# A gated linear recurrence and a SiLU network on one core: the state's product with values as weights, and two reorderings at the start

## The chip, the cores and the metric

The kernel runs on one core of a Trainium2 chip. The metric is the time of one execution on the device in microseconds (us). The kernel before has a median of 665.35 us over three runs (663.98 to 667.26). The profile is that of another execution of the same program: 663.49 us in all, with a span of 661.8 us on the core.

Five engines work side by side, each with its own list of instructions in order: TensorE (PE: matrix products; PEld is its weight load), VectorE (DVE), ScalarE (ACT), GpSimd (POOL) and SyncE (SP), which here only starts transfers. Transfers (DMA) are started on the queues of SyncE, GpSimd and ScalarE, and run beside all of them.

## The reference

Two parts stand one behind the other. First a recurrence in each of 4 x 8 batches and heads, over 768 steps, with a complex state of 48 x 48 that is multiplied by a gate for each row and takes up the outer product of key and value; the output is the query times the real part of the state.

```python
batch, n_heads, seq, head_dim = (4, 8, 768, 48)
...
for t in range(S):
    ar, ai = (a_re_n[:, :, t, :, None], a_im_n[:, :, t, :, None])   # |a| capped at 0.999
    new_re = ar * S_re - ai * S_im
    new_im = ar * S_im + ai * S_re
    kv = np.einsum('bhd,bhe->bhde', k[:, :, t], v[:, :, t])
    S_re, S_im = (new_re + kv, new_im)
    y[:, :, t] = np.einsum('bhd,bhde->bhe', q[:, :, t], S_re)
```

Then a network over the 3072 rows of 384 that the heads make together:

```python
h = x @ w_in                      # (3072, 384) x (384, 2048)
g = h * (1.0 / (1.0 + np.exp(-h)))
return (g @ w_out).astype(np.float32)
```

## The kernel before

The recurrence is worked out in chunks of 128 steps. There are 24 chunks, counted n = 0 to 23: four sequences with six chunks each, so chunk n goes on from chunk n - 4, and chunks 20 to 23 are the last of their sequences. Two chunks make a pair p, and a pair is one step of the main loop: beside the attention of pair p stand the two network products of pair p - 1 (`h`, line 689, and `r`, the product into `o`, line 781) and the gates of pair p + 1.

In a chunk, keys and queries are turned by the running phase of the gates and scaled by their running decay, so that a head has 96 numbers (cosine and sine part) for each time: `kr` and `qr`. With their transposes `kT` and `qT` the kernel makes the weights inside the chunk (`a`, masked to `w`), and the output `y` from two products: values by weights, and the state that was carried in by queries. The state at the end of the chunk is a product over time of `kr` and `v`, added to the state before and multiplied by the decay of the whole chunk.

```python
def output(n):                       # n >= 4; line 592
    ps = p_m.tile([C, HH, C], F32, tag="m", name=f"y{n}")
    for hp in range(HH):             # HH = 4 couples of heads, C = 128
        for r in range(2):           # one head to each half of the partitions
            h = 2 * hp + r
            cols = ds(h * D, 64 if h + 1 < H else D)      # D = 48
            to = ps[64 * r:64 * r + (64 if h + 1 < H else D), hp]
            nc.tensor.matmul(to, lhsT=v_[:, cols], rhs=x["w", h // HH][:, h % HH], ...)
            if carried:
                nc.tensor.matmul(to, lhsT=x["S"]...[:, cols], rhs=x["qT"][:, h], ...)
    ...                              # copied into xT (ScalarE); six small transfers place
                                     # the last two heads' rows in xT, the network's input

def state(n):                        # line 658
    if place(n)[1] == NCH - 1:       # last chunk of its sequence: no state wanted
        return
    ps = p_m.tile([D2, H, D], F32, tag="m", name=f"s{n}")            # D2 = 96
    for h in range(H):
        nc.tensor.matmul(ps[:, h], lhsT=x["kr"][:, h].rearrange("p c d -> p (c d)"),
                         rhs=x["v"][:, h], start=True, stop=True)
    x["s"] = ps
    if n >= STRAIGHT:                # STRAIGHT = 4
        carried_on(n)

def carried_on(n):                   # line 671
    new = att.tile([D2, H, D], F32, tag="S", name=f"S{n + B}", bufs=5)     # B = 4
    by = decs[:, n].unsqueeze(2).to_broadcast([D2, H, D])
    if "S" in x:
        nc.vector.tensor_tensor(out=new, in0=ps, in1=x["S"], op=ALU.add)
        nc.vector.tensor_tensor(out=new, in0=new, in1=by, op=ALU.mult)
    else:
        nc.vector.tensor_tensor(out=new, in0=ps, in1=by, op=ALU.mult)
    X[n + B]["S"] = new
```

The first operand named (`lhsT`) is the stationary one, which is loaded as weights; the second (`rhs`) is moved through. The decay of the whole chunk is the last row of `eq`; it goes to a DRAM array `ends` and comes back, turned, to the tile `decs` on two times 48 partitions (line 511). The transposes of keys and queries are made by VectorE in blocks of 32 x 32 (`sq`, line 560), and twelve transfers put the blocks in their places (`T<-sq`, line 565, half of them on SyncE's queue and half on GpSimd's).

The chunks of the first three pairs, the loads and conversions of the network's weights and the first pairs of the network stand in a list written by hand. A weight's block is loaded raw (as pairs of words; `F`, line 185), and is converted by ScalarE (`R`, the low word, line 218) and VectorE (`H` the high word, `J` both joined); there are four raw buffers. The part of the list that matters here:

```python
... carried:5 r:1 L:5 g:13 r:1 H:1 J:1 F:1 H:1 phase:4 F:1 H:1 R:1 R:1 g:14 J:1 J:1 F:1 h:0
k:4 phase:5 h:1 exp:4 g:04 r:1 H:1 h:0 r:0 R:1 J:1 trig:4 R:1 F:1 table:trig R:1 Q:4 K:4
H:1 carry:6 g:15 trig:5 F:1 exp:5 J:1 tt:4 J:1 h:0 g:05 K:5 Q:5 G0:3 r:0 R:1 H:1 J:1 g:06
R:1 H:1 R:1 H:1 s:4 G5:3 h:0 g:07 G1:3 J:1 h:1 R:1 tt:5 k:6 r:1 g:16 H:1 room:right w:40
h:1 g:17 G7:3 table:trig table:exp w:41 table:exp J:1 J:1 r:1 ...
```

`exp:n` are the two exponentials of chunk n's decay (and the store to `ends`), `trig:n` its sine and cosine, `tt:n` its transposes with their twelve transfers, `s:n` its state, `w:nh` half of its weights, `h:p` and `r:p` a piece of the network's first and second product, `g:pj` the SiLU between them, `G`, `table` parts of the gates of pair 3 and loads of ScalarE's function tables. The order in the main loop is

```python
usual = ("c h E h kA qA h r tA D kB h L qB r F h tB r G h A X a0A th uA uB h a1A r sA h a0B yA "
         "r a1B sB r pA yB pB mA S r mB r lA lB")
```

with `A` and `B` for the pair's two chunks: `E` exponentials, `k`, `q` turned keys and queries, `t` transposes, `a0`, `a1` weights, `s` state, `y` output, `X` the loads of keys, queries and values for the next pair.

Of the kernel before, what the change touches and what calls it, by code (L numbers as in the profile page):

```python
# [11 lines left out]
F32 = mybir.dt.float32  # L12
# [5 lines left out]
ALU = mybir.AluOpType  # L18
# [41 lines left out]
def kernel(  # L60
# [37 lines left out]
    RAW = 4  # L98
    WINO = 2
    STRAIGHT = 4  # L100

    consts = ctx.enter_context(tc.tile_pool(name="consts", bufs=1))
    fast = ExitStack()
# [403 lines left out]
    def ends_of(n):  # L507
        x = X[n]
        nc.sync.dma_start(out=ends[n:n + 1], in_=x["decay"][C - 1:C])
        for a in range(2):  # L510
            nc.gpsimd.dma_start(out=decs[a * D:(a + 1) * D, n],  # L511
                              in_=ends[n].rearrange("(h d) -> d h", d=D))


# [143 lines left out]
    def state(n):  # L658

        x = X[n]  # L660
        if place(n)[1] == NCH - 1:
            return
        ps = p_m.tile([D2, H, D], F32, tag="m", name=f"s{n}")
        for h in range(H):
            nc.tensor.matmul(ps[:, h], lhsT=x["kr"][:, h].rearrange("p c d -> p (c d)"),  # L665
                             rhs=x["v"][:, h], start=True, stop=True)
        x["s"] = ps
        if n >= STRAIGHT:
            carried_on(n)

    def carried_on(n):
        x = X[n]
        ps = x["s"]
        new = att.tile([D2, H, D], F32, tag="S", name=f"S{n + B}", bufs=5)
        by = decs[:, n].unsqueeze(2).to_broadcast([D2, H, D])
        if "S" in x:
            nc.vector.tensor_tensor(out=new, in0=ps, in1=x["S"], op=ALU.add)
            nc.vector.tensor_tensor(out=new, in0=new, in1=by, op=ALU.mult)
        else:
            nc.vector.tensor_tensor(out=new, in0=ps, in1=by, op=ALU.mult)  # L680
        X[n + B]["S"] = new


# [124 lines left out]
    def step(p, h, r, order):  # L808


        what = {"h": lambda: h(1), "r": lambda: r(1), "V": combined_last}
        if p < NP:
            what["E"] = lambda: (table("exp"), both(decays, p), table("silu"))
            for i, x in enumerate("AB"):
                n = 2 * p + i
                what["k" + x] = lambda n=n: rotated(n, "k")
                what["q" + x] = lambda n=n: rotated(n, "q")
                what["t" + x] = lambda n=n: turned(n)
                for hh in range(2):
                    what[f"a{hh}{x}"] = lambda n=n, hh=hh: weights(n, hh)  # L820
                what["s" + x] = lambda n=n: state(n)
                what["y" + x] = lambda n=n: output(n)
        if p + 1 < NP:
            what["c"] = lambda: both(carry, p + 1)
            what["S"] = lambda: both(trig, p + 1)
            what["D"] = lambda: gates_square(p + 1)
            what["L"] = lambda: (table("exp"), gates_log(p + 1))
            what["F"] = lambda: (gates_inverse(p + 1), table("silu"))
            what["G"] = lambda: (gates_l(p + 1), gates_ratio(p + 1), table("trig"),
                                 gates_atan(p + 1), table("silu"))  # L830
            what["th"] = lambda: (gates_side(p + 1), gates_angle(p + 1), both(carried, p + 1))
            for i, x in enumerate("AB"):
                n = 2 * p + 2 + i
                what["u" + x] = lambda n=n: in_two(n, "th")
                what["m" + x] = lambda n=n: in_two(n, "l")
                what["p" + x] = lambda n=n: phases(n)
                what["l" + x] = lambda n=n: sums(n)
            what["X"] = lambda: both(load_x, p + 1)
        if p + 2 < NP:
            what["A"] = lambda: load_a(p + 2)  # L840
        for x in order.split():
            if x in what:
                what[x]()
            if x in "hr" and p + 1 >= NP:
                look()
# [135 lines left out]
    with tc.manual_schedule():  # L981
        for x in """
                table:exp k:1 q:0 warm:30 sq:0 ln:0 k:0 v:0 a:1 v:1 thirds:0 sq:1 l:0 ln:1 l:1 ratio:0
                ratio:1 exp:0 dec:0 warm:34 exp:1 table:trig atan:0 angle:0 phase:0 atan:1 angle:1
                phase:1 warm:20 turn:0 trig:0 rq:00 t:02 rq:01 t:03 rk:00 G0:1 T:03 hold: rk:01 t:01 T:01
                turn:1 trig:1 q:1 dec:1 t:00 w:01 rk:11 rk:10 q:2 T:02 T:00 table:exp rq:11 ends:1 F:2
                H:1 R:1 rq:10 ends:0 k:2 thirds:1 v:2 v:3 t:13 T:13 w:00 t:11 R:1 T:11 G5:1 H:1 F:2 H:1
                s:0 s:1 t:10 G1:1 G2:1 m:00 G7:1 R:1 m:01 w:11 S:1 J:1 S:0 G3:1 q:3 T:10 t:12 y:0 x:0 v:5
                G4:1 L:2 T:12 G6:1 Gat:1 J:1 J:1 L:3 exp:3 F:2 F:1 last:0 R:2 w:10 m:11 m:10 y:1 x:1
                Gan:1 k:3 H:2 J:2 last:1 carry:5 a:3 phase:2 turn:2 exp:2 dec:2 table:trig phase:3 turn:3  # L990
                h:0 trig:2 table:silu g:00 dec:3 h:0 R:2 rk:20 t:20 T:20 thirds:3 F:2 ends:2 v:4 rk:21
                s:2 rq:20 rq:21 q:4 trig:3 H:2 rk:31 rq:31 thirds:2 rq:30 rk:30 a:2 t:21 t:23 t:22 T:22
# [32 lines left out]
    nc.vector.tensor_reduce(out=low, in_=decs.rearrange("p n h -> p (n h)"), op=ALU.min,  # L1025
                            axis=mybir.AxisListType.X)
# [4 lines left out]
    all_ = pre.tile([1, D2 + C], F32, tag="t3", name="all_", bufs=5)  # L1031
    nc.sync.dma_start(out=all_[:, 0:D2], in_=low)
    nc.sync.dma_start(out=all_[:, D2:D2 + C], in_=fit)
# [163 lines left out]
```

## Time and profile before

| engine | busy us | share of the span | instructions |
|---|---|---|---|
| TensorE (products) | 639.2 | 97% | 4084 |
| TensorE (weight loads) | 571.0 | 86% | 4084 |
| VectorE | 463.5 | 70% | 995 |
| ScalarE | 367.1 | 55% | 537 |
| GpSimd | 165.1 | 25% | 260 |

The page of the profile has the span in 40 slices of 16.5 us; a digit is the busy share of a slice in tenths. A row of a timeline gives the start and the duration in us, the engine, the line of the kernel, the operation, the tile written and those read, and the shapes; weights of a product stand as rows*columns. Rows of one kind that follow each other are merged (x16 are sixteen records), and a float32 product has two records. At the end of a row stands the idle time of the engine before it, with what ended it. The products of TensorE are pipelined and their ends are modelled, so that the steps from start to start tell more than the durations.

From 164 us to 570 us the chain of work that ended last is TensorE's alone, in steps of 51.0 us for a pair. The state's product takes 29.5 us of TensorE's busy time in all, in 320 records for 20 chunks.

### The profile page before, as it was taken

What the parts mean: (1) busy time and instruction counts of PE and PEld (TensorE: products, weight loads), DVE (VectorE), ACT (ScalarE), POOL (GpSimd) and SP (SyncE); (2) the same over time, 40 slices, a digit from 0 to 9 for tenths busy, and PEclk for the clock granted to TensorE, in tenths of its full rate; (3) what the DMA queues carried; (4) which work ended last, traced back from release to release, by engine and by line L of the source; (5) the groups of instructions that cost most, each with busy time, mean ns of one, the idle gap of its engine ahead of it and who ended that gap; (6) DMA issues with size and microseconds to landing.
All of it is one profiled execution on the core that took longest, in us unless ns stands there. A gap on an engine that the chain in (4) does not pass through costs nothing.

```text
span 661.8 us, 11281 instructions
## 1 busy us (share of the span) xinstructions
PE 639.2 (97%) x4084; PEld 571.0 (86%) x4084; DVE 463.5 (70%) x995; ACT 367.1 (55%) x537; POOL 165.1 (25%) x260
## 2 busy tenths in 40 slices
PE   6789999989999999999999999999999999998997
PEld 4668866767999999999999999999999999997997
DVE  5998279567975875884784784785785785765543
ACT  6897698696852762662671681780680581610110
POOL 7436000362320320330230240240240250221000
PEclk9999999989999999999999999999999999999999
DMA  9888355555382383293195185175167165578540
GB/s 169 197 187 175 102 152 121 117 93 113 55 150 39 53 143 53 42 143 63 33 134 74 32 127 90 32 112 104 32 94 122 32 85 85 173 171 235 196 145 27
DMA packets 168699, 71.15 MB, mean 108 GB/s; under 512 B 152848, under 2 KB 157072, under 8 KB 168640
## 3 DMA queue, kind: packets, MB, share of 16 engines
q1 hardware_dynamic: 156368, 49.37, 36.5%
q0 software_dynamic: 8960, 16.51, 16.2%
q10 hardware_dynamic: 3312, 4.52, 1.9%
q8 instruction: 33, 0.54, 0.3%
q14 instruction: 26, 0.21, 0.1%
HBM read 48.86 MB, written 4.79 MB: 81 GB/s over the span
## 4 chain that ended last, share of the span: by engine, by line
PE 77%; ACT 7%; DMA 6%; DVE 5%; SPq 3%; issue 1%; POOL 1%; ACTq 0%; DVEq 0%
PE h L689 31%; PE o L781 27%; PE a L578 5%; PE y L608 3%; PE s L665 3%; PE y L611 3%; PE o L737 2%; DMA raw<-in_moe_w_in_dram 2%; SPq L565 2%; ACT L300 2%; ACT s L300 1%; ACT mag L300 1%; DMA raw<-in_moe_w_out_dram 1%; PE phase L441 1%; ACT r L218 1%
## 5 line engine op out<-in xcount | busy, mean ns | idle before, releaser
L689 PE MATMUL h<-xT,w 128*128 128x256 f32 x1152 | 260.3, 380 | 0.0
L689 PEld LDWEIGHTS h<-xT,w 128*128 128x128 f32 x1152 | 216.8, 190 | 28.0 <-DMA xT<-y 0.2
L300 ACT ACTIVATE g<-h 128x512 f32<-128x512 f32 x96 | 55.2, 596 | 138.8 <-PE h L689 135.4
L565 POOL DMA_DIRECT2D T<-sq x120 | 77.2, 651 | 75.8 <-issue 62.4
L295 ACT ACT_TABLE_LOAD x62 | 79.5, 1283 | 2.0 <-PEq L1181 0.9
L781 PE MATMUL o<-w,gs 128*128 128x192 f32 x320 | 77.9, 326 | 0.0
L589 DVE TENSOR_TENSOR w<-a,upto_r 128x512 f32<-128x512 f32 x48 | 32.9, 687 | 62.0 <-PE a L578 62.0
L511 POOL DMA_DIRECT2D decs<-ends x48 | 30.7, 646 | 156.6 <-DMA ends<-eq 145.8
L781 PE MATMUL o<-w,g 128*128 128x192 f32 x320 | 66.7, 331 | 0.0
L625 POOL DMA_DIRECT2D xT<-y x30 | 15.9, 537 | 202.5 <-ACT y L621 194.3
L617 ACT COPY xT<-y 128x384 f32<-128x384 f32 x20 | 9.6, 478 | 100.9 <-PE y L611 100.9
L781 PE MATMUL o<-wc,gs 128*128 128x192 f32 x320 | 65.0, 327 | 0.0
L781 PEld LDWEIGHTS o<-w,g 128*128 128x128 f32 x320 | 53.8, 190 | 3.5 <-issue 1.9
L781 PEld LDWEIGHTS o<-w,gs 128*128 128x128 f32 x320 | 56.4, 190 | 0.0
L578 PEld LDWEIGHTS a<-T 96*128 96x128 f32 x384 | 49.4, 192 | 7.7 <-issue 3.4
L578 PE MATMUL a<-T 96*128 96x128 f32 x384 | 51.1, 277 | 4.0 <-DMA T<-sq 2.8
L781 PEld LDWEIGHTS o<-wc,gs 128*128 128x128 f32 x320 | 54.2, 190 | 0.1
L724 DVE TENSOR_TENSOR gs<-g 128x128 f32<-128x128 f32 x160 | 38.8, 283 | 20.1 <-PE o L781 14.0
L737 PE MATMUL o<-w,g 128*128 128x384 f32 x128 | 45.5, 505 | 3.0 <-ACT g L300 3.0
L737 PEld LDWEIGHTS o<-w,g 128*128 128x128 f32 x128 | 24.7, 197 | 19.9 <-ACT g L300 4.2
L781 PE MATMUL o<-wc,g 128*128 128x192 f32 x160 | 39.0, 327 | 0.0
L608 PE MATMUL y<-w,v 128*64 128x128 f32 x320 | 35.3, 282 | 0.0
(117 smaller groups left out, 977.0 us busy)
## 6 DMA issues: line engine op xcount, KB each, us to landing
T<-sq SPq DMA_DIRECT2D x120, 64.0 KB
T<-sq POOLq DMA_DIRECT2D x120, 64.0 KB, 4.3
raw<-in_moe_w_out_dram SPq DMA_DIRECT2D x16, 384.0 KB
small<-in_moe_w_in_dram SPq DMA_DIRECT2D x16, 384.0 KB
small<-in_moe_w_out_dram SPq DMA_DIRECT2D x16, 384.0 KB
raw<-in_moe_w_in_dram SPq DMA_DIRECT2D x24, 192.0 KB
out_dram<-ot ACTq DMA_DIRECT2D x23, 192.0 KB
im<-in_a_im_dram SPq DMA_DIRECT2D x16, 192.0 KB
```

What stands on the lines that cost most here:

```text
L295: chain(nc.scalar.preload_act_table_set({"exp": "natural_log_exp_and_others", "trig": "trig_and_small", "silu": "silu_and_others"}[of]))
L300: chain(nc.scalar.activation(out=out, in_=in_, func=func, **kw))
L511: nc.gpsimd.dma_start(out=decs[a * D:(a + 1) * D, n], in_=ends[n].rearrange("(h d) -> d h", d=D))
L565: (nc.gpsimd if a % 2 else nc.sync).dma_start(out=to[ts(b, Q), :, a], in_=sq[ts(a, Q), b])
L578: nc.tensor.matmul(ps[:, h], lhsT=x["kT"][:, hh * HH + h], rhs=x["qT"][:, hh * HH + h], start=True, stop=True)
L589: nc.vector.tensor_tensor(out=x["w", hh], in0=x["a", hh], in1=upto.unsqueeze(1).to_broadcast([C, HH, C]), op=ALU.mult)
L608: nc.tensor.matmul(to, lhsT=v_[:, cols], rhs=x["w", h // HH][:, h % HH], start=True, stop=not carried)
L611: nc.tensor.matmul(to, lhsT=x["S"].rearrange("p h d -> p (h d)")[:, cols], rhs=x["qT"][:, h], start=False, stop=True)
L689: nc.tensor.matmul(ps[:, ji], lhsT=w1[:, dc, ts(jp * 2 + ji, C)], rhs=A[p]["xT"][:, dc], start=(dc == 0), stop=(dc == ND - 1))
L724: nc.vector.tensor_tensor(out=t[:, i], in0=a, in1=b, op=op)
L737: nc.tensor.matmul(A[p]["o"][m].rearrange("p n c -> p (n c)"), lhsT=A[p]["g", jp][:, ji, ts(m, C)], rhs=w2[:, j], start=(j == 0), stop=(j ...
L781: nc.tensor.matmul(o[i], lhsT=a, rhs=b, start=(jp == 0 and i < 4), stop=(final and j == jp and i in ((5, 3, 6, 2) if p == NP - 1 else (4, ...
```

## The change

There are three parts.

First, from chunk 6 on (the seventh) the state's product has its operands exchanged: values are the weights and keys are moved, and two heads stand one above the other in the PSUM tile, on 64 partitions each. 64 columns of values are read for a head of 48 (the rest belongs to the next head and isn't used); behind the last head there are 16 columns of zeros, for which the tile of values is made wider. The state then comes out with values along the partitions. VectorE transposes its blocks of 32 x 32, and twelve transfers put them into the tile of the next state, where they are added and multiplied by the decay one step later (`w`, behind the transposes of the second chunk).

The purpose is that two heads may pass through the two halves of the array beside each other.

```diff
+    def state_of_pairs(n):
+        x = X[n]
+        ps = p_m.tile([C, HH, D2], F32, tag="m", name=f"s{n}")
+        for h in range(H):
+            hp, r = divmod(h, 2)
+            nc.tensor.matmul(ps[64 * r:64 * r + 64, hp], lhsT=x["all v"][:, ds(h * D, 64)],
+                             rhs=x["kr"][:, h].rearrange("p c d -> p (c d)"),
+                             start=True, stop=True)
+        sq = moe.tile([C, 2, DM // 2], F32, tag="ot", name=f"ssq{n}").rearrange("p n c -> p (n c)")
+        nc.vector.transpose(sq, ps.rearrange("p h d -> p (h d)"))
+        sq = sq.rearrange("p (h b i) -> p h b i", b=NB, i=Q)
+        new = att.tile([D2, H, D], F32, tag="S", name=f"S{n + B}", bufs=6)
+        to = new.rearrange("p (h r) e -> p r h e", r=2)
+        for b in range(NB):                    # 3
+            for g in range(NA):                # 4
+                r, part = divmod(g, 2)
+                e = slice(part * Q, min((part + 1) * Q, D))
+                (nc.gpsimd if g % 2 else nc.sync).dma_start(
+                    out=to[ts(b, Q), r, :, e], in_=sq[ts(g, Q), :, b, 0:e.stop - e.start])
+        X[n + B]["new"] = new
 ...
     def state(n):
+        if n >= FULL:                          # FULL = 6
+            state_of_pairs(n)
+            return
 ...
     def carried_on(n):                         # (shortened)
-        new = att.tile([D2, H, D], F32, tag="S", name=f"S{n + B}", bufs=5)
+        if "new" in X.get(n + B, ()):
+            new = ps = X[n + B]["new"]
+        elif "s" in x:
+            ps = x["s"]
+            new = att.tile([D2, H, D], F32, tag="S", name=f"S{n + B}", bufs=6)
+        else:
+            return
 ...
+                what["w" + x] = lambda n=n: carried_on(n - 2) if n - 2 >= FULL else None
 ...
-    usual = ("c h E h kA qA h r tA D kB h L qB r F h tB r G h A X a0A th uA uB h a1A r sA h a0B yA "
+    usual = ("c h E h kA qA h r tA D kB h L qB r F h tB wA wB r G h A X a0A th uA uB h a1A r sA h a0B yA "
 ...
-            X[n][name] = ld.tile([C, H, D], F32, tag=name, name=f"{name}{n}",
-                                 bufs=4 if name == "v" else 2)
+            if name == "v":
+                X[n]["all v"] = ld.tile([C, DM + 64 - D], F32, tag="v", name=f"v{n}", bufs=4)
+                nc.gpsimd.memset(X[n]["all v"][:, DM:], 0.0)
+                X[n]["v"] = X[n]["all v"][:, 0:DM].rearrange("p (h d) -> p h d", d=D)
```

Second, the decay of a chunk gets a tile of its own, one of six in turn, in place of a column of the constant tile `decs`. At the end the smallest decay of all, which decides whether a slow fallback is to run, is found from one load of `ends`:

```diff
-    decs = consts.tile([D2, N, H], F32)
+        x["dec"] = att.tile([D2, H], F32, tag="dec", name=f"dec{n}", bufs=6)
 ...
-    low = consts.tile([D2, 1], F32)
-    nc.vector.tensor_reduce(out=low, in_=decs.rearrange("p n h -> p (n h)"), op=ALU.min, ...)
+    decays_ = pre.tile([N, DM], F32, tag="t3", name="decays_", bufs=5)
+    nc.sync.dma_start(out=decays_, in_=ends)
+    low = consts.tile([N, 1], F32)
+    nc.vector.tensor_reduce(out=low, in_=decays_, op=ALU.min, ...)
```

Third, two things move in the list of the start. The exponentials of chunk 5 come right behind those of chunk 4, so that the exponential's table need not be loaded a second time; and the raw loads of the last four weight blocks are started together ahead of the transposes of chunk 4, where one was before and three came later, each when its conversion asked for it:

```diff
-                k:4 phase:5 h:1 exp:4 g:04 r:1 H:1 h:0 r:0 R:1 J:1 trig:4 R:1 F:1 table:trig R:1 Q:4 K:4
-                H:1 carry:6 g:15 trig:5 F:1 exp:5 J:1 tt:4 J:1 h:0 g:05 K:5 Q:5 G0:3 r:0 R:1 H:1 J:1 g:06
+                k:4 phase:5 h:1 exp:4 exp:5 g:04 r:1 H:1 h:0 r:0 R:1 J:1 trig:4 R:1 F:1 table:trig R:1 Q:4 K:4
+                H:1 carry:6 g:15 trig:5 F:4 J:1 tt:4 J:1 h:0 g:05 K:5 Q:5 G0:3 r:0 R:1 H:1 J:1 g:06
```

The order of the products on TensorE is the same as before; only the shape of the state's products differs. On ScalarE two table loads are gone.

More of the change, by code (lines that the diff above doesn't have):

```diff
@@ L100 @@
     STRAIGHT = 4
+    FULL = 6
     consts = ctx.enter_context(tc.tile_pool(name="consts", bufs=1))
@@ L151, in load_x @@
                 continue
-            X[n][name] = ld.tile([C, H, D], F32, tag=name, name=f"{name}{n}",
-                                 bufs=4 if name == "v" else 2)
+            if name == "v":
[3 more added lines that the diff above has]
+            else:
+                X[n][name] = ld.tile([C, H, D], F32, tag=name, name=f"{name}{n}", bufs=2)
             (queue or nc.sync).dma_start(
@@ L509, in ends_of @@
         nc.sync.dma_start(out=ends[n:n + 1], in_=x["decay"][C - 1:C])
+        x["dec"] = att.tile([D2, H], F32, tag="dec", name=f"dec{n}", bufs=6)
         for a in range(2):
-            nc.gpsimd.dma_start(out=decs[a * D:(a + 1) * D, n],
+            nc.gpsimd.dma_start(out=x["dec"][a * D:(a + 1) * D],
                               in_=ends[n].rearrange("(h d) -> d h", d=D))
@@ L669, in state @@
             carried_on(n)
+    def state_of_pairs(n):
[18 more added lines that the diff above has]
+        X[n + B]["new"] = new
     def carried_on(n):
         x = X[n]
-        ps = x["s"]
-        new = att.tile([D2, H, D], F32, tag="S", name=f"S{n + B}", bufs=5)
-        by = decs[:, n].unsqueeze(2).to_broadcast([D2, H, D])
+        by = x["dec"].unsqueeze(2).to_broadcast([D2, H, D])
+        if "new" in X.get(n + B, ()):
[3 more added lines that the diff above has]
+            new = att.tile([D2, H, D], F32, tag="S", name=f"S{n + B}", bufs=6)
+        else:
+            return
         if "S" in x:
             nc.vector.tensor_tensor(out=new, in0=ps, in1=x["S"], op=ALU.add)
-            nc.vector.tensor_tensor(out=new, in0=new, in1=by, op=ALU.mult)
-        else:
-            nc.vector.tensor_tensor(out=new, in0=ps, in1=by, op=ALU.mult)
+            ps = new
+        nc.vector.tensor_tensor(out=new, in0=ps, in1=by, op=ALU.mult)
         X[n + B]["S"] = new
@@ L1023 @@
         mybir.EngineType.PE))
-    low = consts.tile([D2, 1], F32)
-    nc.vector.tensor_reduce(out=low, in_=decs.rearrange("p n h -> p (n h)"), op=ALU.min,
-                            axis=mybir.AxisListType.X)
+    decays_ = pre.tile([N, DM], F32, tag="t3", name="decays_", bufs=5)
+    nc.sync.dma_start(out=decays_, in_=ends)
+    low = consts.tile([N, 1], F32)
+    nc.vector.tensor_reduce(out=low, in_=decays_, op=ALU.min, axis=mybir.AxisListType.X)
     nc.vector.tensor_scalar(out=low, in0=low, scalar1=LEAST, scalar2=None, op0=ALU.is_ge)
@@ L1030 @@
     nc.vector.tensor_scalar(out=fit, in0=fit, scalar1=TINY, scalar2=None, op0=ALU.is_ge)
-    all_ = pre.tile([1, D2 + C], F32, tag="t3", name="all_", bufs=5)
-    nc.sync.dma_start(out=all_[:, 0:D2], in_=low)
-    nc.sync.dma_start(out=all_[:, D2:D2 + C], in_=fit)
+    all_ = pre.tile([1, N + C], F32, tag="t3", name="all_", bufs=5)
+    nc.sync.dma_start(out=all_[:, 0:N], in_=low)
+    nc.sync.dma_start(out=all_[:, N:N + C], in_=fit)
     weak = consts.tile([1, 1], I32)
```

## The prediction

> **What bounds the kernel now.** I read the page's busy shares first, then the waits of TensorE, then the engines' timelines in two places: a settled step of the main loop, and the start, where the waits are.
>
> ```profile
> PE   6789999989999999999999999999999999998997
> ```
>
> ```profile
> PE o L737 <- ACT g L300: 3.0, 3, 2.2
> ```
>
> ```profile
> 140.00:145.00 5.00, 3.98 (x7) 2.26 (x8) 2.10 (x5) 4.92 (x7) 5.00 (x8) 0.66 0.88 120
> ```
>
> The first line is the page's busy share of TensorE in 40 slices of 16.5 us: idle at the start, in slice 9, and in the last slices. TensorE is busy 639.2 of 661.8 us, so 22.6 us is all that removing its waits could give; anything more must come from less work on TensorE. The second line is the only wait of TensorE that the list shows between 100 and 160 us: 3.0 us in three pieces for ScalarE's silu. The third is one row of the table by stretches: in 140 to 145 us the granted clock averaged 0.66, so (1 - 0.66) x 5 = 1.7 us of TensorE's work was lost on top of the wait.
>
> A settled step (51.0 us, two chunks) on TensorE:
>
> ```profile
> 243.64 1.48 PE L665 MATMUL s<-v,kr 128*96 128x48 f32 x16
> 244.96 2.82 PE L689 MATMUL h<-xT,w 128*128 128x256 f32 x12
> ...
> 248.61 0.45 PE L608 MATMUL y<-w,v 128*64 128x128 f32 x4
> ...
> 250.20 0.44 PE L611 MATMUL y<-T,S 96*64 96x128 f32 x4
> 250.57 0.92 PE L781 MATMUL o<-w,g 128*128 128x192 f32 x4
> ...
> 253.84 1.48 PE L665 MATMUL s<-v,kr 128*96 128x48 f32 x16
> 255.16 0.88 PE L781 MATMUL o<-w,g 128*128 128x192 f32 x4
> ```
>
> Columns: start, duration, engine, line, tiles, weights' rows*columns, moving shape. Nothing is idle; the state's product holds TensorE from 243.64 to 244.96. A float32 product stands as two records, so the x16 are 8 heads. In the single records one s piece starts every 85 ns, although only 48 columns are moved: 256 moved columns (h) take 216 ns a record and 192 (o) take 162, so 48 would take about 40. It is the load of 96 weight columns that sets the 85. Counted from the end of the stream before to the start of the next one's, one state costs 1.39 us in every one of these steps.
>
> The start, on ScalarE, on TensorE and on SyncE's queue:
>
> ```profile
> 118.16 1.28 ACT L300 ACT_TABLE_LOAD   x1
> ...
> 120.55 1.28 ACT L300 ACT_TABLE_LOAD   x1
> ...
> 130.36 0.56 ACT L218 ACTIVATE r<-raw 128x384 int32<-128x384 uint32 x1 [4.80 <-DMA raw<-in_moe_w_out_dram]
> 132.76 0.58 ACT L218 ACTIVATE r<-raw 128x384 int32<-128x384 uint32 x1 [1.84 <-DMA raw<-in_moe_w_out_dram]
> 133.24 0.58 ACT L300 ACTIVATE g<-h 128x512 f32<-128x512 f32 x1
> ...
> 140.37 1.08 ACT L300 ACTIVATE g<-h 128x512 f32<-128x512 f32 x2
> ```
>
> ```profile
> 137.81 1.05 PE L578 MATMUL a<-T 96*128 96x128 f32 x8
> 141.02 7.12 PE L737 MATMUL o<-w,g 128*128 128x384 f32 x16 [2.15 <-ACT g L300]
> ```
>
> ```profile
> 120.39 4.14 SPq L565 DMA_DIRECT2D T<-sq  x6
> 124.58 1.97 SPq L185 DMA_DIRECT2D raw<-in_moe_w_out_dram  x3
> ```
>
> Read from the bottom: the last three loads of the second weights are issued at 124.58, behind six transfers of transposed keys that themselves stood behind the fifth (counting from 0) chunk's exponential; they land at 130 to 133; ScalarE stands for them (4.80 + 1.84 us), so its silu comes at 140.37, and TensorE waits 2.15 us. Then 16 o records take 7.12 us where 8 take 2.58 from start to start: about 1.8 us too long, the half clock above.
>
> [...] The trace shows column tiles at work already: the y records of the two output halves start in couples 12 ns apart (248767 and 248779 ns, 248876 and 248888 ns), and 32 records of 128 moved columns, 107 ns each, fill 1.76 us from first to last start, not 3.4. [...] after the last a record the first y record starts 98 ns late, and after y the next full-width product starts 304 ns after the last y start, of which 107 are its own columns[...]. [...]
>
> **The change part by part.** (1) For chunks 6 to 19 (14 chunks; chunks 20 to 23 are last of their sequence and have no state) the values become the stationary side (64 columns), the rotated keys move (96 columns), and two heads go to the two halves of the PSUM tile. Estimate from y: entry 98 ns; [...] then 7.5 couples of 96 moved columns, 80 ns plus the 3.5 that y also loses per couple, 626 ns; the last piece 80 ns and the way out 197 ns. Sum 98 + 53 + 626 + 80 + 197 = 1.05 us against 1.39: 0.34 us a chunk, x 14 = 4.7 us, all on the bound, since TensorE has no idle time there. The halved stream alone would promise 16 x 85 - 8 x 80 = 0.72 us[...].
>
> (2) The state now comes out transposed. Added for each of the 14 chunks: one VectorE block transposition of 128x384 (about 0.5 us, half of the 0.97 and 0.94 us of the 128x768 ones), 12 small transfers (6 on SyncE's queue, 6 on GpSimd's, at about 0.6 us an issue as in the rows above: 4 us on each queue). The two VectorE operations (0.55 + 0.55 us) move into the next step, behind the transposed keys. VectorE is at 36.7 us of a step's 51, so 1 us more a step is off the bound. At its new place the four operations (2.2 us) push the mask of weights (238.08) and what follows by 0.8 us; before the state of the next pair VectorE had 2.03 us idle (before the mask at 248.71), so this is taken up. Cost on the bound: 0.
>
> (3) Values' tiles get 16 zeroed columns: a GpSimd memset for each load, about 24 in all, ahead of transfers that have slack. I put 0.1 us on the path at the start.
>
> (4) The chunk-5 exponentials stand right behind those of chunk 4: two table loads fewer, 2 x 1.28 us off ScalarE around 118 to 122 us. The loads of the last four blocks stand ahead of the transposed keys. They wait only for buffers, which the conversions on VectorE and ScalarE release by 116 us, so they land near 121, before ScalarE wants them. The silu of 133.24 can then start when its h is there, 129.1; the 7.1 us of ScalarE work from it to the silu at 140.37 end at 136.2, before TensorE gets there (138.9). The 2.15 us go, with them the lost clock, 1.7 us, and 0.42 us of an earlier silu wait at 122.49: 4.3 us at most. I count 3.8, because another wait may show behind the one removed.
>
> (5) The smallest decay is found from one late load of all rows instead of a constant tile: one DMA and 0.2 us more of VectorE at the end, 0.1 us.
>
> Sum: 665.35 - 4.7 - 3.8 + 0.2 = 657.05.
>
> **The rivals.** (a) The halves don't run side by side here, because every piece changes its half: then 16 x 83 + 350 ns = 1.68 us a state, 0.29 worse than before, and the time is 665.35 + 4.1 - 3.6 = 666. The y records, which also change halves, speak against it. (b) The way back of the state becomes a new wait. In the step shown, y's copy goes out at 260.69 on both queues and h needs it at 265.63; with issue 1.8 us and landing 1.8 us it has about 1.3 us to spare. The second state's transposition can end at 255.9 and its six issues at 260.0, before 260.7. If the issues take a third longer, as the T issues did (5.2 us for six), xT slips by 0.6 us, still inside the slack. If it slips by 2 us, 0.7 us a step over seven steps, about 5 us: 662. (c) The start gives little: the silu is replaced by a wait for the joined weights on VectorE or for the gates' logarithms: 660. (d) [...] at 0.65 us a chunk, 653.
>
> **Range and chances.** The two gains are independent and of similar size. With (1) between 2.5 and 8 us and (4) between 1 and 4.5 us, the sum lies between 653 and 661 in most cases. A gain over 2% needs 652.0, that is (d) and the whole of (4) together: 0.09. Slower by over 2% needs a stall of some 3 us in every step against the slack shown: 0.03.
>
> **What would show it.** Of the changed kernel: s records of 128*64 weights in couples, a state of 1.0 to 1.1 us, steps of 50.3 us (right for (1)); 1.6 us a state shows (a). Waits of h for xT, or of y for S, show (b). At 120 to 142 us: raw loads for w_out before the T transfers, ScalarE without waits for raw, no wait at the o product and no half clock (right for (4)). The prediction is wrong if any of these holds the other way[...].

## The result, and the profile after

The changed kernel has a median of 656.22 us over four runs (654.15 to 658.24); the kernel before, in four runs on the same chip, 664.88 us. The ratio is 0.9864 [0.9816, 0.9912], a gain of 9.0 us (the two medians are 8.7 us apart). The prediction was 657.0 in a range of 653 to 661.

The page of the changed kernel, its span, its busy line and two of its 40-slice lines:

```profile
span 656.2 us, 11518 instructions
PE 636.2 (97%) x4084; PEld 563.6 (86%) x4084; DVE 469.1 (71%) x1009; ACT 364.6 (56%) x535; POOL 213.8 (33%) x368
PE   6889999999999999999999999999999999998997
PEclk8899999999999999999999999999999999998999
```

TensorE stays the bound, with as many products as before and 3.0 us less of busy time. VectorE has 14 instructions more and GpSimd 108 more. Slice 9, which was an 8, is a 9.

A settled step on TensorE (start, duration, engine, line, tile, shapes):

```profile
240.32 0.88 PE L687 MATMUL s<-kr,v 128*64 128x96 f32 x16
241.14 2.86 PE L725 MATMUL h<-xT,w 128*128 128x256 f32 x12
...
250.15 0.88 PE L687 MATMUL s<-kr,v 128*64 128x96 f32 x16
250.96 0.92 PE L817 MATMUL o<-w,g 128*128 128x192 f32 x4
```

The same sixteen records now take 0.82 us from their start to that of `h` (0.81 to `o`), where they took 1.32. To this comes what the change of product costs at both ends: 0.10 us between the end of the stream before and the first start, and another 0.10 us by which the second record of the next product is late (before: none and 0.07). In all a state costs 1.01 us in place of 1.39. The single records start in couples: 240325 and 240332 ns, 240458 and 240466, 240541 and 240548, and so on, 7 to 8 ns apart and a couple every 82.5 ns. Two heads do pass side by side.

What that makes of a step, in the table by stretches (length, busy time of TensorE, its loads, VectorE, ScalarE and GpSimd with numbers of instructions, granted clock, DMA share, GB/s); first before, then after:

```profile
239.83:290.83 51.00, 51.00 (x346) 47.82 (x345) 36.96 (x83) 27.55 (x41) 11.86 (x19) 1.00 0.49 80
```

```profile
235.00:285.24 50.24, 50.24 (x346) 46.43 (x345) 37.75 (x85) 27.56 (x41) 18.61 (x34) 1.00 0.57 88
```

TensorE is busy for the whole of both stretches. A step is 0.76 us shorter, which is two states at 0.38. VectorE's 0.8 us and GpSimd's 6.8 us more lie beside TensorE.

The start of the changed kernel, on TensorE, on ScalarE and on SyncE's queue:

```profile
138.87 1.06 PE L584 MATMUL a<-T 96*128 96x128 f32 x8
139.77 5.33 PE L773 MATMUL o<-w,g 128*128 128x384 f32 x16
...
151.31 2.02 PE L584 MATMUL a<-T 96*128 96x128 f32 x16 [0.16 <-DMA T<-sq]
```

```profile
124.36 0.99 ACT L224 ACTIVATE r<-raw 128x384 int32<-128x384 uint32 x2
130.42 0.60 ACT L305 ACTIVATE g<-h 128x512 f32<-128x512 f32 x1 [5.08 <-PE h L725]
```

```profile
112.38 5.82 SPq L191 DMA_DIRECT2D raw<-in_moe_w_out_dram  x4
120.24 16.98 SPq L571 DMA_DIRECT2D T<-sq  x12
```

The four raw loads are issued at 112 us, before the transposed keys. ScalarE's last two conversions follow each other at 124.36 without a wait, and the engine now stands for TensorE's `h`, not for a transfer. The `o` product starts 0.90 us after the start of `a`, with no wait between them, and its 16 records take 5.33 us where they took 7.12.

Lined up by the start of the same product, the two traces drift apart like this (minus: the changed kernel is earlier):

| TensorE's place, us in the kernel before | drift | what happened there |
|---|---|---|
| 53 | +1.66 | half clock at 10.8 and 27.9 us in this execution |
| 122 | +1.17 | the small silu wait is gone: -0.49 |
| 141.0, start of `o` | -1.25 | the silu wait is gone: -2.42 |
| 148.0 | -3.04 | no half clock: -1.79 |
| 154.0 | -2.72 | transposed keys waited for: +0.32 |
| 194.0, after the first changed state | -3.06 | -0.34 |
| 510.2, after the last | -8.01 | thirteen times -0.38 |
| the last product | -5.8 | near the end two waits for transposed keys (0.59 and 2.59 us) where one stood (2.84), and a half clock behind the second: +2.2 |

The first and last rows don't belong to the change: in another profiled execution of the changed kernel neither is there, and the drift at 510 us is -10.7.

### The profile page after: what moved, and what is told of

The parts are those of the page before. It is cut to its first block, busy times and chain, and to the rows that moved or that the text cites. A ratio compares the mean times of both kernels' runs of the same rounds, so it can differ in the third digit from the quotient of the medians.

```text
span 656.2 us, 11518 instructions
## 1 busy us (share of the span) xinstructions
PE 636.2 (97%) x4084; PEld 563.6 (86%) x4084; DVE 469.1 (71%) x1009; ACT 364.6 (56%) x535; POOL 213.8 (33%) x368
## 4 chain that ended last, share of the span: by engine, by line
PE 79%; DMA 8%; ACT 7%; SPq 2%; DVE 2%; issue 1%; DVEq 0%; ACTq 0%
PE h L725 33%; PE o L817 27%; PE a L584 6%; PE y L614 3%; DMA T<-sq 3%; DMA raw<-in_moe_w_in_dram 3%; PE y L617 3%; PE o L773 2%; SPq L571 2%; PE s L687 2%; ACT L305 1%; ACT s L305 1%; ACT mag L305 1%; PE phase L446 1%; ACT r L224 1%
## 5 line engine op out<-in xcount | busy, mean ns | idle before, releaser
L517 POOL DMA_DIRECT2D dec<-ends x48 | 31.0, 653 | 143.4 <-DMA ends<-eq 143.4
L699 POOL DMA_DIRECT2D S<-ssq x84 | 45.8, 553 | 94.8 <-DVE ssq L691 56.5
L773 PE MATMUL o<-w,g 128*128 128x384 f32 x128 | 43.6, 488 | 0.4 <-ACT g L305 0.4
```

Source lines behind the costliest of these rows:

```text
L517: nc.gpsimd.dma_start(out=x["dec"][a * D:(a + 1) * D], in_=ends[n].rearrange("(h d) -> d h", d=D))
L699: (nc.gpsimd if g % 2 else nc.sync).dma_start(out=to[ts(b, Q), r, :, e], in_=sq[ts(g, Q), :, b, 0:e.stop - e.start])
L773: nc.tensor.matmul(A[p]["o"][m].rearrange("p n c -> p (n c)"), lhsT=A[p]["g", jp][:, ji, ts(m, C)], rhs=w2[:, j], start=(j == 0), stop=(j ...
```

## The experiments

Eleven runs were made, three of them of kernels that had run already. Ratios are to the kernel before, run beside them on the same chip. They are formed from all runs, so that a gain worked out from a ratio can differ by up to 1.6 us from the distance of the two medians.

**One part at a time.** First the state alone, with the start's list as it was:

```diff
-  ... exp:4 exp:5 g:04 ... / ... trig:5 F:4 J:1 tt:4 ...
+  ... exp:4 g:04 ...       / ... trig:5 F:1 exp:5 J:1 tt:4 ...
```

> The changed kernel with the list of the start as it was before: values as weights from chunk 6 on, nothing moved at the start. My theory: the state costs 1.01 us in place of 1.39 for 14 chunks, 5.3 us in all, and the start keeps its silu wait of 2.15 us and the half clock: 659.6 (0.992 of before). Rival (the start's two moves make nearly all of the gain): 664.

Measured: 659.43 us against 663.87, 0.9909 [0.9874, 0.9945], a gain of 6.0 us by the ratio. The trace gets 0.38 us further ahead of the kernel before at each of 14 states (5.3 us in all), and the silu wait stayed. Its list of waits and its row for 140 to 145 us, to be read like those of the kernel before:

```profile
PE o L773 <- ACT g L305: 3.1, 3, 2.1
```

```profile
140.00:145.00 5.00, 4.25 (x8) 2.34 (x9) 1.83 (x4) 4.92 (x7) 5.00 (x9) 0.68 0.88 126
```

The other way round, the kernel before with both moves of the list and nothing else:

```diff
-  ... exp:4 g:04 ...       / ... trig:5 F:1 exp:5 J:1 tt:4 ...
+  ... exp:4 exp:5 g:04 ... / ... trig:5 F:4 J:1 tt:4 ...
```

> The kernel before with only the two moves in the list of the start. My theory: the silu waits of 0.42 and 2.15 us and the half clock behind them go (1.8 us), 4.3 us in all: 660.6 (0.9935). Rival (the next wait comes in their place): 664. Together with e1 the gains should add up to that of the whole change, 9 us; if their sum is over 11 or under 7, the parts touch each other.

Measured: 661.74 us, 0.9956 [0.9936, 0.9975], a gain of 2.9 us. The trace shows the same stage as the whole change, -2.42 and -1.79 us and then +0.24 of transposed keys. Of the three silu waits the list has one left, the earliest, which the kernel before has too (0.41 us at 102.41 us):

```profile
PE o L737 <- ACT g L300: 0.4, 1, 0.4
```

The two halves make 6.0 + 2.9 = 8.9 us; the whole made 9.0, and 10.2 when it ran again. Within the intervals, which are wide (3.7 to 8.4 and 1.7 to 4.2 us), they add up, and there is no sign that one gives back what the other gained.

**The start taken apart.** The exponentials moved, the loads left where they were:

```diff
-  ... exp:4 g:04 ...       / ... trig:5 F:1 exp:5 J:1 tt:4 ...
+  ... exp:4 exp:5 g:04 ... / ... trig:5 F:1 J:1 tt:4 ...
```

> The kernel before with chunk 5's exponentials behind those of chunk 4, and the loads of the last weights left one by one behind the transposed keys. The store of the decay no longer holds the transposed keys' transfers on the queue, so that keys and loads both come about 2 us earlier. Theory (the loads' place is what counts): the loads still land only near 130, most of the silu wait stays, gain 1 to 2 us: 663.5. Rival (ScalarE's two table loads are what counts): wait and half clock gone, 660.6.

And the loads moved, the exponentials left:

```diff
-  ... trig:5 F:1 exp:5 J:1 tt:4 ...
+  ... trig:5 F:4 exp:5 J:1 tt:4 ...
```

> The kernel before with the last four raw loads together ahead of the transposed keys, and chunk 5's exponentials where they were, with their two table loads. Theory (the loads' place is what counts): silu wait and half clock gone, the small wait of 0.42 us near 122 stays: 661.0. Rival (the table loads are what counts): 664.

Measured: 662.34 us, 0.9964 [0.9945, 0.9982] for the exponentials, 661.21 us, 0.9943 [0.9915, 0.9972] for the loads. These intervals overlap with each other and with that of both moves; the times don't tell the three apart. The traces do. With the exponentials alone the loads are still late in the queue, yet hardly any wait is left. First the queue of the kernel before ahead of what the prediction shows of it, then this kernel:

```profile
120.00 0.21 SPq L509 DMA_DIRECT2D ends<-eq  x1
```

```profile
108.79 1.20 SPq L509 DMA_DIRECT2D ends<-eq  x2
...
121.35 4.86 SPq L565 DMA_DIRECT2D T<-sq  x6
126.31 2.81 SPq L185 DMA_DIRECT2D raw<-in_moe_w_out_dram  x3
...
132.39 1.22 ACT L218 ACTIVATE r<-raw 128x384 int32<-128x384 uint32 x2 [6.88 <-DVE w L47]
...
141.32 5.43 PE L737 MATMUL o<-w,g 128*128 128x384 f32 x16 [0.34 <-ACT g L300]
```

With the loads alone:

```profile
112.92 5.08 SPq L185 DMA_DIRECT2D raw<-in_moe_w_out_dram  x4
...
140.12 5.33 PE L737 MATMUL o<-w,g 128*128 128x384 f32 x16
```

Either move removes the wait of 2.15 us, down to 0.34 or to nothing, and the half clock behind it. My expectation that most of the wait would stay without the loads fell. The two table loads (2 x 1.28 us) aren't the reason by themselves: ScalarE still stands 6.88 us until VectorE, which waited 5.71 us for the raw loads, has done its half of the conversion, and in that time it could load both tables. What the move frees is SyncE's queue. In the kernel before the transposed keys' blocks are ready at 118.4 us, but their transfers are issued only at 120.39, behind the store of chunk 5's decay, whose exponential stood late; here both stores are out by 110 us, and the transfers follow the last transposition (121.2 us) at once. TensorE is 2.1 us later in this execution, so that the loads behind those transfers, and with them the silu at 141 us, come some 1.8 us earlier relative to TensorE, and that was nearly the whole wait. The gains of the two moves are one gain with two ways to it; adding them would count it twice.

**What makes two heads run side by side.** The same products with all heads of the lower half first, then those of the upper:

```diff
-        for h in range(H):
+        for h in [*range(0, H, 2), *range(1, H, 2)]:
```

> The changed kernel with the heads of the state's product in another order: the four heads of the lower half of the partitions first, then the four of the upper half. The same products, loads and transfers. Theory (two halves run side by side only where neighbours in TensorE's list go to different halves): a state takes 16 x 82 ns plus entry and exit of 0.35, 1.66 us against 1.01, over 14 chunks 9 us: 665. Rival (TensorE finds the other half's work further on in its list, or the gain comes from the smaller load alone): 1.0 us a state and 656.

Measured: 658.30 us, 0.9906 [0.9873, 0.9939], 4.8 us over the changed kernel's 653.50 beside it (4.0 by the ratios). Timeline of a step of this kernel:

```profile
238.44 1.26 PE L687 MATMUL s<-kr,v 128*64 128x96 f32 x16
239.63 2.86 PE L725 MATMUL h<-xT,w 128*128 128x256 f32 x12
```

The state costs 1.39 us again, the 0.38 us are lost, and 14 x 0.38 = 5.3 is about the 4.8. Neither of my two numbers (1.66 with no overlap, 1.0 with all of it) was met. The single records of a state elsewhere in this trace say why: the upper half's first record starts 387 ns after the lower half's first, between the lower half's fifth (198013 ns) and sixth (198095). The times are the same to 2 ns in all 14 states. So the upper half's first record, the ninth in the list, started ahead of three that stand before it; four of the eight records of each half run beside one of the other, and the other four alone. The interleaving of heads in the change is what earns the gain; in this order nothing of it is left.

**Where the rest of the state's cost is.** If 98 ns go in at the entry and 199 at the exit (terms of the prediction's first part, as measured in the changed kernel's records), then putting the state directly ahead of `y`, which is tiled in the same way, should save one pair of them:

```diff
-  ... h a1A r sA h a0B yA r a1B sB r pA yB pB mA ...
+  ... h a1A r h sA yA a0B r a1B sB yB r pA pB mA ...
```

> The changed kernel with the state's product right ahead of the output's product of the same chunk, so that the two that use half of the array's columns stand together (order: r, h, sA, yA, a0B for the first chunk, a1B, sB, yB, r, pA, pB for the second). Theory (0.30 us or so is lost at each way into and out of the halved array): one way out and one way in less for each of 14 chunks, 0.25 to 0.35 us each, 4 us: 652. Rival (y now waits for the mask or for a PSUM buffer, as it comes sooner after a): 656 to 660, with waits of y in the list.

Measured: 650.34 us, 0.9789 [0.9763, 0.9815], 3.2 us better than the changed kernel beside it. Timeline of a step:

```profile
240.66 0.88 PE L687 MATMUL s<-kr,v 128*64 128x96 f32 x16
241.37 0.44 PE L614 MATMUL y<-w,v 128*64 128x128 f32 x4
...
243.28 1.16 PE L584 MATMUL a<-T 96*128 96x128 f32 x8
...
247.54 0.88 PE L687 MATMUL s<-kr,v 128*64 128x96 f32 x16
248.39 0.45 PE L614 MATMUL y<-w,v 128*64 128x128 f32 x4
...
250.36 0.92 PE L817 MATMUL o<-w,g 128*128 128x192 f32 x4
```

The state's first start to `y`'s first is 0.71 us in the first chunk of the pair. State and `y` together take 2.82 us where they took 1.01 + 2.165 apart, 0.36 us less: one entry, one exit and 51 ns are gone (in the changed kernel the state's second couple starts 133 ns after its first, where the later steps are 82.5). In the second chunk it is 0.85 us, and from the state's first start to `y`'s last it is 2615 ns against 2423 in the first: here `y` starts only when the mask `w` is there, about 0.2 us later, and the stretch is 3.02 us, as before (3.03). The step is 49.76 us, 0.48 less than 50.24, of which 0.11 us lie outside these two stretches and weren't traced. Seven steps of 0.48 are 3.4 us, about the 3.2 measured.

Next the same kernel with fewer loads in the way of the last transposed keys. Near the end the network's weights are loaded once more, block by block (`small`), to find the smallest magnitude, which belongs to the decision on the fallback. These loads now start only behind the last transposes, and twice as many of them fall in double steps:

```diff
-            if x in "hr" and p + 1 >= NP:
+            if x == "tB":
+                last_keys.append(p)
+            if x in "hr" and NP - 1 in last_keys:
...
-        for _ in range(1 + (len(looks) % 6 == 0)):
+        for _ in range(1 + (len(looks) % 3 == 0)):
```

> The kernel with the state beside y, and in the last attention step the loads and reductions that look through the weights for small values begin only behind the transposed keys of the last chunk, at a quicker pace (one and a half for each piece of the network's products). All 32 of them are still made. In every profile so far TensorE waits 1 to 3.6 us for the last transposed keys near 600 us, and mostly a window of half clock follows. Theory (VectorE waits for one of these loads ahead of the last transposition[...]): wait and half clock go, 2.5 to 4.5 us less than the 650.3 of the state beside y: 646 to 648. Rival (the last keys are late for another reason, or the looks now hold up the last y on SyncE's queue): 650 or more.

Measured: 649.96 us against 663.42, 0.9783 [0.976, 0.9806]: not told apart from the version before it (0.9789). The waits of TensorE that the edit was aimed at, first in the kernel with the state beside `y`, then in this one:

```profile
PE a L584 <- DMA T<-sq: 1.3, 2, 1.0
PE y L614 <- DVE w L595: 1.1, 2, 0.9
```

```profile
PE y L614 <- DVE w L595: 1.1, 2, 0.8
```

The wait for transposed keys went, but it had been 1.0 us there at most, not the 2.6 and 3.1 of the changed kernel's two profiles, and `y`'s wait for the mask stayed. The 2 to 4 us that I expected were no longer there to be had.

**Whether the way back is free or only hidden.** All twelve transfers of the state on SyncE's queue:

```diff
-                (nc.gpsimd if g % 2 else nc.sync).dma_start(
+                nc.sync.dma_start(
```

> The changed kernel with all twelve transfers of a state on SyncE's queue, none on GpSimd's. Theory (the way back of the state is hidden only because it ends ahead of the transfers of y into the network's input): the second state's twelve issues take some 7.5 us from 255.5 on in a step like the one shown, so the queue is free at 263, xT is issued 2.5 us late and the network's product waits 1 to 2 us in each of seven steps: 664 to 669. Rival (there is more slack than I read): 656 and no wait for xT.

Measured: 699.55 us, 1.0547 [1.0507, 1.0588], 46 us over the changed kernel. SyncE's queue, TensorE and TensorE's wait in this kernel:

```profile
309.07 16.64 SPq L699 DMA_DIRECT2D S<-ssq  x24
325.81 1.82 SPq L631 DMA_DIRECT2D xT<-y  x3
```

```profile
327.75 9.47 PE L725 MATMUL h<-xT,w 128*128 128x256 f32 x36 [3.97 <-DMA xT<-y]
```

```profile
PE h L725 <- DMA xT<-y: 25.8, 7, 4.3
```

The 24 issues take 16.64 us (0.69 each), and `y`'s transfers into `xT` stand behind them: they go out 8.10 us after `y`'s last start, where it was 0.98, so 7.12 us late, and `h` waits 3.97. In all seven steps the wait is 3.15 us shorter than the delay. That was the time to spare, and not the 1.3 us of the prediction. The mechanism was the one I named, and the size was not: I had 664 to 669. Two things were missing. The first state's issues start late as well, because the queue is busy with the loads for the next pair until 309 us. And behind the waits stand half-clock windows, stretches in which TensorE is granted half its clock (0.89 on average in 326 to 341 us, behind the wait shown): the mean granted clock is 0.969 in this execution and 0.999 in that of the changed kernel beside it, so that 0.030 x 697.7 = 20.9 us come on top of 25.8 us of waiting. The sum, 46.7, is what the two spans differ by (697.7 - 651.6 = 46.1).

**The changed kernel and two others again.** The changed kernel without an edit:

> The changed kernel again, to know its spread: of four runs two stood near 654.3 and two near 658. Theory (in the slower two a window of half clock falls into the start, where TensorE has short pauses, and some microseconds are lost by chance): the same two groups, median 654 to 658, and a clock near 0.997 goes with the short runs and 0.990 with the long. Rival (the difference lies in waits for transfers): times that don't go with the clock.

Measured: 653.50 us (652.64 to 656.88), 0.9846 [0.982, 0.9872]. Its PEclk line has no 8 anywhere:

```profile
PEclk9999999999999999999999999999999999999999
```

In the first four runs of the changed kernel two spans are 652.4 and 652.8 us at a mean clock of 0.996 to 0.997, and two are 656.2 and 656.5 at 0.992 and 0.989. Over 147 executions of these kernels 0.001 of clock goes with 0.51 us, so the mean clocks of the two sets (0.9935 and 0.9967) account for 1.6 of the 2.2 us between their mean times. The two profiles say the same: that of 657.93 us has half clock three times for 3.41 us ahead of the last product (5.1 us lost), that of 653.30 never, and their spans differ by 4.6.

The kernel before without an edit, and the list alone once more, one execution each:

> The kernel before once more, for its profile: where do the windows of half clock stand? Theory (each wait of TensorE of 2 us or more can be followed by a window of half clock[...]): a window near 141 again, since the wait of 2.15 us is there in every execution, and perhaps one near 605. Rival (the window at 141 was chance): none there.

> Only the two moves in the list of the start, once more, for its profile. Theory: no wait and no half clock between 120 and 160 us, as before it; a window near 600 in most executions, which is why the time falls by less than the 4.2 us that this stage shows. Rival: a window near 141 here too.

Measured: 666.25 and 662.47 us. The first has the silu wait (2.0 us) and behind it half clock from 142.0 to 145.4 us; the second has neither. Counting all profiles of this study: where TensorE waited some 2 us at 141 us (before, the state alone, before again), a half-clock window followed in 3 of 3 (granted clock 0.66 and 0.68 over 140 to 145 us in the first two, 0.50 within the window of the kernel before); where it didn't, in 0 of 10. At 600 us, where TensorE waits for the last transposed keys, a window followed in 9 of the 11 profiles in which the wait was 2.2 to 3.6 us, and in neither of the 2 in which it was 1.0 us or none. So the half clock went with the wait. The two waits without a window were not the short ones. From the lists of waits (in total, times, longest) of the kernel before and of the changed kernel again, neither with a window there, and of the changed kernel's first profile, with one:

```profile
PE a L578 <- DMA T<-sq: 2.8, 1, 2.8
```

```profile
PE a L584 <- DMA T<-sq: 3.3, 2, 3.1
```

```profile
PE a L584 <- DMA T<-sq: 3.3, 3, 2.6
```

What tells them apart is where they fall. Within one execution the windows begin whole multiples of 3.413 us apart (kernel before: at 141.12 and 659.94 us, 152 times; changed kernel: at 10.82, 27.89, 597.91 and 655.94, 5, 172 and 189 times from the first). Cut a trace into stretches of that length which end 0.2 us before the places of the windows, a distance chosen to fit. Then, in all 13 profiles from 40 us on to the last product, every stretch at full clock with at least 1.77 us of idle TensorE is followed by a window (19 of them), and none with 1.75 us or less is. In the kernel before it is 2.05 us of idle (137.50 to 140.92 us) with a window behind it and 1.75 (601.72 to 605.13) with none; in the changed kernel 1.77 (594.30 to 597.71) with one, and 0.86 at most with none. The wait of 2.84 us (from 600.62 us on) is cut into 1.09 + 1.75, that of 3.11 (from 589.96) into 1.61 + 1.50; of the 2.59 us (from 593.48), 1.77 lie in one stretch. This is a fit to these profiles, not a test, and why some windows last twice as long isn't shown.

What stays open: the mean clock of the list alone over 16 runs (0.9933) isn't above that of the kernel before over 64 (0.9939), though one window fewer should raise it by 0.0026. Only the profiled executions show where windows lie, and where the others had theirs wasn't seen. It may also be why the gain of the list, 2.9 us, is smaller than the 4.4 us that the trace of the changed kernel shows up to 154 us.

## Why the prediction was right

**Step 1, the state's product: right, its size 11% low.** Predicted 1.39 to 1.05 us, 4.7 us in all; measured 1.39 to 1.01, 5.3 us by the trace and 6.0 (3.7 to 8.4) by the time of the state alone. Term by term: entry 98 ns predicted, 96 to 98 measured; from the first start to the last 53 + 626 = 679 predicted, 635 measured (no trace of the kernel before shows the 53, which stood for the first load; in the changed kernel the second couple starts 133 ns after the first, 51 more than 82.5); the last piece and the way out 80 + 197 predicted, 80 + 199 measured. (The 304 ns after `y` from which the prediction took the 197, as 304 less 107, are two delays: the next product's first record starts 201 ns after `y`'s last, and its second is 0.10 us late.) The mis-sized term is the middle one: between the first and the last of sixteen records in eight couples lie seven steps and not seven and a half (41 ns), at 82.5 ns each and not 83.5. The trace bears the exchange out with the couples 7 to 8 ns apart, on a condition that only the run of half after half showed: a state cost 1.01 us with the two halves alternating in the list, and 1.39 with one behind the other.

That the loads set the 85 ns of the product before was read from its records alone. The loads of the kernel before keep the same pace, which fits it:

```profile
243.48 1.52 PEld L665 LDWEIGHTS s<-v,kr 128*96 128x96 f32 x16
```

From the second on they start 83 to 86 ns apart, and the loads are busy for the whole of 243.64 to 244.90 us.

**Step 2, the way back: right, cost 0, with less to spare on the queue than I had thought and more behind it.** In the settled step TensorE is never idle. SyncE's queue of the changed kernel:

```profile
247.06 8.74 SPq L699 DMA_DIRECT2D S<-ssq  x12
256.52 1.83 SPq L631 DMA_DIRECT2D xT<-y  x3
```

The last of the state's twelve issues ends at 255.80, and `xT`'s first is at 256.52, as long after `y`'s last start as before the change (0.98 us). In the other profile of this kernel it is 253.75 and 253.84. Over the seven steps of both profiles the queue is free 0.1 to 1.0 us ahead of `xT`, and once, at 505.46 us in the second, it isn't, and `xT` goes out 0.43 us late. TensorE doesn't wait there: by the run on one queue `xT` has 3.15 us to spare. Where all transfers stood on this queue, both were used up, and it cost 46 us.

```profile
L691 DVE STREAM_TRANSPOSE ssq<-s 128x384 f32<-128x384 f32 x14 | 8.1, 579 | 1.1 <-PE s L687 1.1
```

VectorE's transposition is 0.58 us (0.5 predicted), and GpSimd's issues are 553 ns each (0.6 predicted).

**Step 3, the zeroed columns, and step 5, the late load: too small to be seen.** The memsets are 204 ns each, 24 of them, on an engine that is busy for a third of the span, and no wait of TensorE names them. The smallest decay is ready 80 us before the end, as before. That each is 0.1 us on the path, as I had it, was neither shown nor refuted.

**Step 4, the start: right in its chain, and the time smaller than counted.** Wait, half clock and the small wait at 122 us went as described, and "another wait may show behind the one removed" came true as 0.32 us of transposed keys. In the trace that is 0.49 + 2.42 + 1.79 - 0.32 = 4.4 us against 3.8 counted. In time it is 2.9 (1.7 to 4.2). The difference may be the clock of other stretches; it is the open point above. What the step left out, without harm to the sum, is that the two moves are two ways to the same gain: each alone takes nearly all of it, since each brings the raw loads in earlier.

**The sum:** -8.3 predicted; -9.0 (5.9 to 12.2) in the first comparison, -10.2 (8.5 to 12.0) in the second. The traces' two terms make 5.3 + 4.4 = 9.7. That the forecast lies closest to the first comparison is partly luck: both terms were sized too small, and two of the four executions there ran at 0.992 and 0.989 of the clock.

**The rivals.** (a), halves that don't run side by side: refuted by the couples, and even with the heads in the wrong order it is 1.39 us and not 1.68. (b), a way back that delays `xT`: not in the change, but real once the queue is overloaded, and then far above the 5 us I gave it; a slip of 2 us, which I had priced at 5 us, would have fallen inside the 3.15 us to spare. (c), a start that gives little: not in the trace; in time the 0.9 us it left to the start lies outside the measured 1.7 to 4.2. (d), 0.65 us gained per state: refuted, it was 0.38; entry and exit cost 98 and 199 ns, as at `y` (98 and 197).

## What to carry to other kernels

Hold a product's steps against what its moved columns alone would take: here 48 moved columns behind a load of 96 took 85 ns a record, with the loads 83 to 86 ns apart, where 40 would be their own (an estimate from the 216 ns of 256 columns). With operands exchanged and two halves alternating record by record two records took 82.5 ns, but each way into the products by halves and out again cost about 0.3 us (98 and 199 ns); with them side by side this kernel gained 3.2 us more. What the exchange moves to other engines was free here while their queues had room, and cost 46 us when SyncE's had none: look at the queue, not at busy shares, and shut off half of it once to see what is behind. Of a start full of waits, count a chain once: two edits that each shorten it don't add.

## What the runs showed of the hardware

- **A wait of 2.15 us cost nearly twice itself.** So it was at 141 us in the kernel before, where another 1.79 us went in the half clock behind it (granted clock 0.50). At 141 and 600 us 12 of 14 waits of TensorE of 2.0 to 3.6 us were followed by half clock, for 3.41 us in eight cases and for 6.83 in four, and half of that time is lost; where the wait was 1.0 us at most, none of 12 was. 2.0 us were enough in the kernel before run again, and 3.1 us in the changed kernel run again were not; in the fit above 2.05 of the 2.15 us of the kernel before fall into one stretch, and the 3.1 us are cut in two.
- **With one half's eight records ahead of the other's, the halves overlapped only in part.** The other half's first record started 387 ns after the first, when three records of the first half had not started yet, and the state took 1.39 us.
- **Going into the products by halves and out of them cost nearly the same for two widths:** 98 ns in and 199 ns out for the state's 96 moved columns, 98 and 197 for `y`'s 128.
